# Row-tiled fill in batches 1 and 2, and moved block borders in the fill of batches 3 to 7

## The chip, the cores and the metric

The kernel runs on one core of a Trainium2 chip. The metric is device time in microseconds (us), as the median of several executions. Single slow executions (over 1.5% above the fastest of their kernel) are left out of the ratios.

## The reference

Attention with a decay of forgetting, for 8 batches of 8 heads, 576 positions and head dimension 64, feeds a two-layer network with an exact GELU.

```python
scores = matmul(q, k.T) / 8 + cum[:, None] - cum[None, :]   # cum = cumsum(log f), causal
x = softmax(scores) @ v                                     # (8, 8, 576, 64)
x = x.transpose(0, 2, 1, 3).reshape(4608, 512)
h = x @ w_in                                                # 512 -> 2048
out = gelu(h) @ w_out                                       # 2048 -> 512
```

## The kernel before

The program interleaves two things on TensorE. While the attention of batch b waits for exp on ScalarE, TensorE computes the second GEMM of batch b-1. That work is called the **fill**. A unit of fill, a step, is one contraction tile of 128 rows, taken either as one full-height matmul ("n") or as two row tiles of 64 rows ("r") that write two different banks of PSUM (the memory that TensorE writes its results to) and run side by side. The scores have 64 rows too (head dimension 64), so "r" steps stand beside scores without a change of TensorE's tiling mode. AV (the product with V), the transposes of x and the first GEMM use 128 rows.

Heads go in pairs, four pairs to a batch. A pair has four score tiles, t = 0 to 3. After each tile some fill steps are taken, and AV of the pair before comes between the tiles. There are three PSUM pools of two buffers each: "s" for scores, "o" for AV, "m" for the rest.

```python
    def scores(b, i, t):
        on_pe = b == 0 or (b == 1 and i == 0)   # causal mask as matmuls; else on GpSimd
        ...
        nc.scalar.activation(et[:, :, z:c], st[:, :, z:c], Act.Exp, scale=scale)
        for c0 in [] if on_pe else SDIAG[t]:
            nc.gpsimd.affine_select(...)

    def to_xT(b, i, copy, pool=m_psum, tag="m", ps=None):
        ...                                     # a bank ps, from the pool named
        for m in range(NBLK):
            nc.tensor.transpose(ps[:, m * P : (m + 1) * P], x_of[b, i][:, m, :, :], ident_bf)
        copy(xT(b)[:, i, :], ps)
```

The fill of batches 3 to 7 follows PLAN, token block by token block. Each block holds two banks, and ends with a copy of one and an add of the other on VectorE. FILL says how many steps follow each score tile.

```python
    PLAN = [
        (0, "o", 16 * "r"),
        (1, "m", 6 * "r" + "n" + 9 * "r"),
        (2, "m", "n" + 9 * "r" + "n" + 5 * "r"),
        (3, "s", 7 * "r" + 9 * "n"),
    ]
    FILL = [[7, 6, 3, 3], [1, 3, 3, 3], [1, 3, 3, 3], [1, 3, 3, 3], [7]]
    FILL_1 = [[0, 0, 0, 0], [0, 0, 0, 0], [2, 2, 2, 2], [2, 2, 2, 2]]   # batch 1
```

In batch 1 the fill is the first half of the contraction of two token blocks of batch 0, in full-height matmuls. The second half of that contraction comes at the start of batch 2.

```python
    def gemm2_half(c, half):
        pss = [m_psum.tile([P, d_model], FP32, tag="m", name="ps2") for _ in range(2)]
        k0, k1 = half * n_ff // 2, (half + 1) * n_ff // 2
        if half:
            order = [(ts, kt) for ts in range(2) for kt in range(k0, k1)]
        else:       # contraction tiles 0-3 of both blocks, then 4-7 of both
            order = [(ts, kq + kt) for kq in (0, 4) for ts in range(2) for kt in range(4)]
        ...         # one full-height matmul per step; evictions by VectorE and ScalarE

    def second_attention():
        ...
        for i in range(HP):
            for t in range(4):
                scores(b, i, t)
                ...
                take(fill, FILL_1[i][t])
                if i and t in (1, 2):
                    av(i - 1, t - 1)                    # one head after tile 1, one after 2
                if i > 1 and t == 0:
                    to_xT(b, i - 2, nc.vector.tensor_copy, o_psum, "o")
                ...
        to_xT(b, HP - 2, nc.vector.tensor_copy, o_psum, "o")
        av(HP - 1, 0)
        av(HP - 1, 1)
        both = s_psum.tile([P, 2, 1024], BF16, tag="s", name="ps_x2")
        gemm1_begin(1, both)                            # first GEMM starts after the last AV
        x_tail(1); load_w_out(2); load_w_out(3); load_v(2)
```

The softmax here doesn't subtract the row's maximum and nothing guards it: scores larger than these inputs give would overflow.

Of the kernel before, what the change touches and what calls it, by code (L numbers as in the profile page):

```python
# [8 lines left out]
FP32 = mybir.dt.float32  # L9
BF16 = mybir.dt.bfloat16  # L10
Act = mybir.ActivationFunctionType
Alu = mybir.AluOpType
PSUM = bass.MemoryType.PSUM

P = 128
# [37 lines left out]
def kernel(  # L53
# [214 lines left out]
    e_of = {}  # L268

    def scores(b, i, t):  # L270
        on_pe = b == 0 or (b == 1 and i == 0)
        st = s_psum.tile([P, 2, 512], FP32, tag="s", name=f"s{t}")
        c = 0
        for n, q0, w in STILES[t]:
            z = D if n == NBLK - 1 else 0
            masked = on_pe and c in SDIAG[t]
            for half in range(-1, 2 if masked else 0):
                if half == 0 and z:
                    continue
                for h in range(2):  # L280
                    d = slice(h * D, (h + 1) * D)
                    if half < 0:
                        to = st[:, h, c + z : c + w]
                        ab = kT[i][d, K0[n] : K0[n] + P], qT[i][d, q0 + z : q0 + w]
                    else:
                        last = (half + 1) * D
                        to = st[:, h, c + z : c + last]
                        ab = key_of[d, half, :], after[d, half, z:last]
                    nc.tensor.matmul(  # L289
                        to, *ab, start=half < 0, stop=half == 1 or not masked  # L290
                    )
            c += w
        z = D if t == 1 else 0
        if z:
            et = e4[(b * HP + i) % len(e4)]
        else:
            et = e_pool.tile([P, 2, 512], BF16, tag=f"e{t}", name=f"e{t}")
        e_of[b, i, t] = et
        nc.scalar.activation(et[:, :, z:c], st[:, :, z:c], Act.Exp, scale=scale)  # L299
        for c0 in [] if on_pe else SDIAG[t]:  # L300
            nc.gpsimd.affine_select(  # L301
                out=et[:, :, c0 + z : c0 + P],
                in_=et[:, :, c0 + z : c0 + P],
                compare_op=Alu.is_ge,
                fill=0.0,
                base=z,
                pattern=[[0, 2], [1, P - z]],
                channel_multiplier=-1,
            )
# [84 lines left out]
    def gemm2(c):  # L394
# [35 lines left out]

    PLAN = [
        (0, "o", 16 * "r"),
        (1, "m", 6 * "r" + "n" + 9 * "r"),
        (2, "m", "n" + 9 * "r" + "n" + 5 * "r"),
        (3, "s", 7 * "r" + 9 * "n"),
    ]

# [42 lines left out]
    def store(c, ts, ot):  # L480
        nc.sync.dma_start(out[c * S + ts * P : c * S + (ts + 1) * P, :], ot)
# [2 lines left out]

    def gemm2_half(c, half):

        pss = [
            m_psum.tile([P, d_model], FP32, tag="m", name="ps2") for _ in range(2)
        ]
        k0, k1 = half * n_ff // 2, (half + 1) * n_ff // 2  # L490
        if half:
            order = [(ts, kt) for ts in range(2) for kt in range(k0, k1)]
        else:
            order = [
                (ts, kq + kt)
                for kq in (0, 4)
                for ts in range(2)
                for kt in range(4)
            ]
        for ts, kt in order:  # L500
            nc.tensor.matmul(  # L501
                pss[ts],
                g_of[c][kt][:, ts * P : (ts + 1) * P],
                w_out_sb[:, kt, :],
                start=(kt == k0),
                stop=(kt == k1 - 1),
            )
            if kt == k1 - 1 and not half:
                ot_of.append(o_pool.tile([P, d_model], FP32, tag="ot", name="ot"))
                (nc.scalar.copy if ts else nc.vector.tensor_copy)(ot_of[ts], pss[ts])  # L510
            elif kt == k1 - 1:
                nc.vector.tensor_tensor(ot_of[ts], ot_of[ts], pss[ts], Alu.add)
                store(c, ts, ot_of[ts])
            yield

    def gemm2_third():
        yield from gemm2_half(0, 1)
        yield from gemm2_rows(0, PLAN_0)
        yield from gemm2_rows(1, PLAN_1)

    def take(gen, n):
# [92 lines left out]



    FILL = [[7, 6, 3, 3], [1, 3, 3, 3], [1, 3, 3, 3], [1, 3, 3, 3], [7]]
    FILL_2 = [[8, 8, 8, 8], [8, 8, 4, 4], [4, 4, 4, 4], [4, 4, 4, 4], [8]]
    FILL_1 = [[0, 0, 0, 0], [0, 0, 0, 0], [2, 2, 2, 2], [2, 2, 2, 2]]

    def attention(b):

# [33 lines left out]
    def second_attention():  # L656
# [16 lines left out]
        for i in range(HP):  # L673
            for t in range(4):
# [1 line left out]
                if i == 0 and t < 3:  # L676
                    transposes(t + 1, *((m_psum, "m") if t == 1 else (o_psum, "o")))
                take(fill, FILL_1[i][t])
                if i and t in (1, 2):
                    av(i - 1, t - 1)  # L680
                if i > 1 and t == 0:
                    to_xT(b, i - 2, nc.vector.tensor_copy, o_psum, "o")
                if (i, t) == (1, 3):
                    load_qk_tokens(2, which="k")
                if (i, t) == (3, 0):
                    transpose_dma(2, 0, 4)
                    transpose_dma(2, 4, 8)
        to_xT(b, HP - 2, nc.vector.tensor_copy, o_psum, "o")
        av(HP - 1, 0)
        av(HP - 1, 1)  # L690
        both = s_psum.tile([P, 2, 1024], BF16, tag="s", name="ps_x2")
        gemm1_begin(1, both)
        x_tail(1)
        load_w_out(2)
        load_w_out(3)
# [66 lines left out]
```

## Time and profile before

The median is 348.33 us (347.60 to 348.62, four executions); the profiled span is 345.7 us. The table gives the lengths of the batches in the trace, from the first score matmul of one to that of the next.

| stretch | before, us |
|---|---|
| batch 1 | 32.60 |
| batch 2 | 46.91 |
| each of batches 3 to 7, mean | 36.15 |

The end of batch 1's attention shows where its waits are. This is the timeline of TensorE: start, length, line, tiles, count, and in brackets idle time with its releaser. In all views PE is TensorE, PEld its weight loads, DVE VectorE, ACT ScalarE, POOL GpSimd and SP SyncE.

```profile
47.07 0.37 PE L289 MATMUL s<-qT,kT 64*128 64x256 bf16 x4 [0.28 <-ACT e L299]
...
55.26 0.31 PE L289 MATMUL s<-qT,kT 64*128 64x320 bf16 x2
...
56.91 0.97 PE L320 MATMUL o<-vw,e 128*128 128x65 bf16 x25 [0.15 <-POOL e L301]
...
72.27 0.37 PE L289 MATMUL s<-qT,kT 64*128 64x256 bf16 x4
```

The first line is the start of pair 2, the second the last score tile of pair 3, the third the last AV waiting for the mask on GpSimd, and the fourth the start of batch 2.

### The profile page before, as it was taken

Reading aid. Unit: us, or ns where it says so; the run is one execution under the profiler, and the core shown is the slowest. Engines: PE = TensorE matmul, PEld = TensorE weight load, DVE = VectorE, ACT = ScalarE, POOL = GpSimd, SP = SyncE. Lnnn points to the kernel's source line nnn. Section 1 sums busy time; section 2 is a strip of 40 time slices with the busy share of each in tenths; the row PEclk is TensorE's granted clock in tenths of the full one; section 3 lists DMA queues with packets and bytes.
Section 4 is the critical chain, followed back from the end, with each engine's and each line's share of the span. In section 5 each row is a group of like instructions: output and inputs, shape, how many; then the busy total and the mean of one; then the engine's idle time right before and its main releaser. Section 6 shows DMA issues by size and latency. Waiting matters only on the chain.

```text
span 345.7 us, 7895 instructions
## 1 busy us (share of the span) xinstructions
PE 328.3 (95%) x3187; PEld 173.7 (50%) x3227; DVE 188.1 (54%) x424; ACT 212.1 (61%) x296; POOL 125.1 (36%) x256
## 2 busy tenths in 40 slices
PE   7899999999999999999899989998999899999995
PEld 3674555445554455545554555445544554444443
DVE  5670456934367935795479647974597542020011
ACT  5976786773634787368746874687468765503600
POOL 8390673128418044533345333624261430000000
PEclk9999999999999999999999999999999999999999
DMA  8999999979992999488935995498900230011013
GB/s 116 176 171 194 202 178 147 170 149 161 222 183 100 138 202 176 81 119 167 219 89 81 134 211 137 74 161 190 170 30 2 69 83 30 2 61 61 0 35 89
DMA packets 99924, 43.03 MB, mean 124 GB/s; under 512 B 78704, under 2 KB 95344, under 8 KB 99888
## 3 DMA queue, kind: packets, MB, share of 16 engines
q1 hardware_dynamic: 82592, 28.37, 42.4%
q0 software_dynamic: 16896, 13.63, 26.9%
q8 instruction: 25, 0.41, 0.5%
q10 hardware_dynamic: 400, 0.52, 0.4%
q14 instruction: 11, 0.09, 0.1%
HBM read 36.85 MB, written 9.44 MB: 134 GB/s over the span
## 4 chain that ended last, share of the span: by engine, by line
PE 89%; DVE 4%; ACT 3%; issue 2%; POOL 2%; POOLq 0%; ACTq 0%; DVEq 0%
PE ps L375 35%; PE ps L466 25%; PE o L320 9%; PE ps L408 8%; PE s L289 8%; ACT e L299 2%; PE ps L501 2%; PE ps_x L353 1%; DVE ot L474 1%; PE ps_f L206 1%; DVE x L334 1%; POOL q L107 1%; POOL k L107 1%; DVE qT L213 0%; DVE kT L213 0%
## 5 line engine op out<-in xcount | busy, mean ns | idle before, releaser
L392 ACT ACTIVATE g<-ps 128x512 bf16<-128x512 f32 x144 | 85.3, 597 | 80.2 <-PE ps L375 80.2
L299 ACT ACTIVATE e<-s 128x896 bf16<-128x896 f32 (+2 forms) x128 | 101.0, 836 | 32.1 <-PE s L289 28.2
L375 PE MATMUL ps<-xT,w_in_sb 128*128 128x512 bf16 x497 | 111.4, 379 | 0.8
L466 PE MATMUL ps<-w_out_sb,g 64*128 64x512 bf16 (+1 forms) x736 | 104.0, 376 | 4.7 <-DVE ot L474 3.9
L375 PEld LDWEIGHTS <-w_in_sb 128*128 128x128 bf16 x576 | 56.0, 98 | 67.5 <-issue 1.8
L301 POOL TENSOR_SCALAR_AFFINE_SELECT e<-e 128x256 bf16<-128x256 bf16 (+1 forms) x135 | 49.5, 385 | 100.1 <-ACT e L299 99.9
L466 PEld LDWEIGHTS <-g 64*128 64x128 bf16 (+1 forms) x756 | 39.8, 94 | 40.4 <-issue 10.6
L244 DVE COPY qT<-tq 64x288 bf16<-64x288 bf16 x96 | 49.3, 514 | 1.4
L260 POOL TENSOR_TENSOR vw<-v_sb,wT 128x640 bf16<-128x640 f32 x31 | 39.6, 1279 | 24.7 <-DMA v_sb<-in_v_dram 24.5
L289 PE MATMUL s<-qT,kT 64*128 64x320 bf16 (+4 forms) x384 | 43.9, 277 | 3.3 <-ACT e L299 2.6
L320 PE MATMUL o<-vw,e 128*128 128x65 bf16 x960 | 36.8, 194 | 2.7 <-issue 2.4
L320 PEld LDWEIGHTS <-e 128*128 128x128 bf16 x960 | 34.8, 98 | 9.2 <-POOL e L301 4.1
L474 DVE COPY ot<-ps 128x512 f32<-128x512 f32 x26 | 17.9, 690 | 35.5 <-PE ps L466 35.5
L244 DVE COPY kT<-tk 64x288 bf16<-64x288 bf16 x96 | 33.0, 344 | 1.6
L334 DVE TENSOR_TENSOR x<-o,r 128x320 bf16<-128x320 f32 x64 | 31.5, 492 | 2.2
L417 DVE COPY ot<-ps 128x512 f32<-128x512 f32 (+2 forms) x9 | 5.7, 632 | 48.8 <-PE ps L408 31.9
L289 PEld LDWEIGHTS <-kT 64*128 64x128 bf16 x384 | 18.7, 94 | 22.6 <-issue 7.3
L333 DVE RECIPROCAL r<-o 128x5 f32<-128x5 f32 x64 | 12.2, 190 | 30.8 <-PE o L320 30.7
L408 PE MATMUL ps<-w_out_sb,g 128*128 128x512 bf16 (+2 forms) x142 | 27.9, 355 | 0.1
L408 PEld LDWEIGHTS <-g 128*128 128x128 bf16 x144 | 13.5, 98 | 14.5
L476 DVE TENSOR_TENSOR ot<-ot,ps 128x512 f32<-128x512 f32 x26 | 17.9, 687 | 1.2
L375 PE MATMUL ps<-tails,w_in_sb 128*128 128x512 bf16 x63 | 14.3, 377 | 0.1
(64 smaller groups left out, 148.2 us busy)
## 6 DMA issues: line engine op xcount, KB each, us to landing
out_dram<-ot SPq DMA_DIRECT2D x32, 256.0 KB, 2.3
v_sb<-in_v_dram SPq DMA_DIRECT2D x24, 256.0 KB, 5.7
q<-in_q_dram POOLq DMA_DIRECT2D x6, 576.0 KB, 6.2
k<-in_k_dram POOLq DMA_DIRECT2D x6, 576.0 KB, 8.2
v_sb<-in_v_dram SPq DMA_DIRECT2D x22, 128.0 KB, 5.3
w_in_sb<-in_moe_w_in_dram POOLq DMA_DIRECT2D x4, 512.0 KB, 7.0
w_out_sb<-in_moe_w_out_dram POOLq DMA_DIRECT2D x4, 512.0 KB, 8.4
q<-in_q_dram POOLq DMA_DIRECT2D x4, 144.0 KB, 4.5
```

Source lines behind the costliest of these rows:

```text
L244: nc.vector.tensor_copy(rows[:, odd], src[odd * D : (odd + 1) * D, 2 * i + h].rearrange("d j p -> d p j"),)
L260: eng.tensor_tensor(vw_of[b][:, hs, :, 0:D], v_sb[:, hs, :, :], w.unsqueeze(3).to_broadcast([P, 2, NBLK, D]), Alu.mult,)
L289: nc.tensor.matmul(to, *ab, start=half < 0, stop=half == 1 or not masked)
L299: nc.scalar.activation(et[:, :, z:c], st[:, :, z:c], Act.Exp, scale=scale)
L301: nc.gpsimd.affine_select(out=et[:, :, c0 + z : c0 + P], in_=et[:, :, c0 + z : c0 + P], compare_op=Alu.is_ge, fill=0.0, base=z, pattern=[[ ...
L320: nc.tensor.matmul(o[:, m, :], e_of[b, i, t][:, h, c : c + P], vw_of[b][:, 2 * i + h, n, :], start=(n == 0), stop=(n == m),)
L334: nc.vector.tensor_tensor(x_of[b, i][:, :, h, :], o[:, :, 0:D], r.unsqueeze(2).to_broadcast([P, NBLK, D]), Alu.mult,)
L375: nc.tensor.matmul(ps, w_in_sb[:, kt, ffb * P : (ffb + 1) * P], src[:, kt, 0:TC], start=(kt == 0), stop=(kt == n_dm - 1),)
L392: nc.scalar.activation(g_of[c][ffb], ps, Act.Gelu)
L408: nc.tensor.matmul(pss[ts][:, c0:c1], g_of[c][kt][:, ts * P : (ts + 1) * P], w_out_sb[:, kt, c0:c1], start=(kt == 0), stop=(kt == n_ff - 1),)
L466: nc.tensor.matmul(banks[r], g_of[c][kt][rows, ts * P : (ts + 1) * P], w_out_sb[rows, kt, :], start=kt == (steps.index("r") if r else 0), ...
L474: nc.vector.tensor_copy(ot, banks[1])
```

## The change

It has three parts. (a) In the steady fill (batches 3 to 7) the borders of the token blocks move to the AV runs, so that the eviction of a finished block lies under AV. (b) In batch 2 the second half of the split contraction becomes row tiles, and the order of its blocks changes. (c) In batch 1 the fill becomes row tiles too. So that AV and the transposes stand together in 128-row mode, both heads' AV and the x transpose move to tile 2; the last mask goes from GpSimd to TensorE; and four matmuls of the first GEMM are begun ahead of the last AV.

```diff
--- before.py
+++ after.py
@@ -268,7 +268,7 @@
     e_of = {}
 
     def scores(b, i, t):
-        on_pe = b == 0 or (b == 1 and i == 0)
+        on_pe = b == 0 or (b == 1 and (i == 0 or (i, t) == (HP - 1, 3)))
         st = s_psum.tile([P, 2, 512], FP32, tag="s", name=f"s{t}")
         c = 0
         for n, q0, w in STILES[t]:
@@ -430,8 +430,8 @@
 
     PLAN = [
         (0, "o", 16 * "r"),
-        (1, "m", 6 * "r" + "n" + 9 * "r"),
-        (2, "m", "n" + 9 * "r" + "n" + 5 * "r"),
+        (1, "m", 6 * "r" + "n" + 8 * "r" + "n"),
+        (2, "m", 9 * "r" + "n" + 6 * "r"),
         (3, "s", 7 * "r" + 9 * "n"),
     ]
 
@@ -484,38 +484,42 @@
 
     def gemm2_half(c, half):
 
-        pss = [
-            m_psum.tile([P, d_model], FP32, tag="m", name="ps2") for _ in range(2)
-        ]
+
         k0, k1 = half * n_ff // 2, (half + 1) * n_ff // 2
-        if half:
-            order = [(ts, kt) for ts in range(2) for kt in range(k0, k1)]
-        else:
-            order = [
-                (ts, kq + kt)
-                for kq in (0, 4)
-                for ts in range(2)
-                for kt in range(4)
+        for ts in range(2):
+            pool, held = (o_psum, "o") if half and ts else (m_psum, "m")
+            banks = [
+                pool.tile([P, d_model], FP32, tag=held, name="ps2") for _ in range(2)
             ]
-        for ts, kt in order:
-            nc.tensor.matmul(
-                pss[ts],
-                g_of[c][kt][:, ts * P : (ts + 1) * P],
-                w_out_sb[:, kt, :],
-                start=(kt == k0),
-                stop=(kt == k1 - 1),
-            )
-            if kt == k1 - 1 and not half:
-                ot_of.append(o_pool.tile([P, d_model], FP32, tag="ot", name="ot"))
-                (nc.scalar.copy if ts else nc.vector.tensor_copy)(ot_of[ts], pss[ts])
-            elif kt == k1 - 1:
-                nc.vector.tensor_tensor(ot_of[ts], ot_of[ts], pss[ts], Alu.add)
-                store(c, ts, ot_of[ts])
-            yield
+            for kt in range(k0, k1):
+                for r in range(2):
+                    rows = slice(r * D, (r + 1) * D)
+                    nc.tensor.matmul(
+                        banks[r],
+                        g_of[c][kt][rows, ts * P : (ts + 1) * P],
+                        w_out_sb[rows, kt, :],
+                        start=(kt == k0),
+                        stop=(kt == k1 - 1),
+                    )
+                if kt == k1 - 1:
+                    if not half:
+                        ot_of.append(
+                            o_pool.tile([P, d_model], FP32, tag="ot", name="ot")
+                        )
+                        nc.vector.tensor_copy(ot_of[ts], banks[0])
+                    else:
+                        nc.vector.tensor_tensor(
+                            ot_of[ts], ot_of[ts], banks[0], Alu.add
+                        )
+                    nc.vector.tensor_tensor(ot_of[ts], ot_of[ts], banks[1], Alu.add)
+                    if half:
+                        store(c, ts, ot_of[ts])
+                yield
 
     def gemm2_third():
+        yield from gemm2_rows(0, PLAN_0[:1])
         yield from gemm2_half(0, 1)
-        yield from gemm2_rows(0, PLAN_0)
+        yield from gemm2_rows(0, PLAN_0[1:])
         yield from gemm2_rows(1, PLAN_1)
 
     def take(gen, n):
@@ -614,9 +618,9 @@
 
 
 
-    FILL = [[7, 6, 3, 3], [1, 3, 3, 3], [1, 3, 3, 3], [1, 3, 3, 3], [7]]
+    FILL = [[7, 6, 3, 3], [1, 3, 3, 2], [1, 3, 3, 3], [1, 3, 3, 3], [8]]
     FILL_2 = [[8, 8, 8, 8], [8, 8, 4, 4], [4, 4, 4, 4], [4, 4, 4, 4], [8]]
-    FILL_1 = [[0, 0, 0, 0], [0, 0, 0, 0], [2, 2, 2, 2], [2, 2, 2, 2]]
+    FILL_1 = [[0, 0, 0, 0], [0, 0, 0, 2], [2, 2, 2, 2], [2, 2, 2, 0]]
 
     def attention(b):
 
@@ -676,20 +680,36 @@
                 if i == 0 and t < 3:
                     transposes(t + 1, *((m_psum, "m") if t == 1 else (o_psum, "o")))
                 take(fill, FILL_1[i][t])
-                if i and t in (1, 2):
-                    av(i - 1, t - 1)
-                if i > 1 and t == 0:
+                if i == 1 and t in (1, 2):
+                    av(0, t - 1)
+                if i > 1 and t == 2:
                     to_xT(b, i - 2, nc.vector.tensor_copy, o_psum, "o")
+                    av(i - 1, 0)
+                    av(i - 1, 1)
                 if (i, t) == (1, 3):
                     load_qk_tokens(2, which="k")
                 if (i, t) == (3, 0):
                     transpose_dma(2, 0, 4)
                     transpose_dma(2, 4, 8)
-        to_xT(b, HP - 2, nc.vector.tensor_copy, o_psum, "o")
+        pss = [gemm1(1, ffb, (0, 1)) for ffb in range(2)]
         av(HP - 1, 0)
         av(HP - 1, 1)
         both = s_psum.tile([P, 2, 1024], BF16, tag="s", name="ps_x2")
-        gemm1_begin(1, both)
+        to_xT(1, HP - 2, nc.vector.tensor_copy, ps=both[:, 0, 0:XC])
+        more = s_psum.tile([P, 2, 512], FP32, tag="s", name="ps1")
+        pss += [more[:, 0, :], more[:, 1, :]]
+        gemm1(1, 2, (0, 1), pss[2])
+        for ffb in range(2):
+            gemm1(1, ffb, (2,), pss[ffb])
+        gemm1(1, 2, (2,), pss[2])
+        to_xT(1, HP - 1, nc.vector.tensor_copy, ps=both[:, 1, 0:XC])
+        gemm1(1, 3, (0, 1, 2), pss[3])
+        for ffb in range(2):
+            gemm1(1, ffb, (3,), pss[ffb])
+        for ffb in (2, 3):
+            gemm1(1, ffb, (3,), pss[ffb], False)
+        gelu(1, 2, pss[2])
+        gelu(1, 3, pss[3])
         x_tail(1)
         load_w_out(2)
         load_w_out(3)
```

## The prediction

> **What bounds the kernel now.** I read the page first (busy shares, chain, groups), then the waits, then the chain in order of time, then the timeline of the stretches that the diff touches.
>
> ```profile
> PE 328.3 (95%) x3187; PEld 173.7 (50%) x3227; DVE 188.1 (54%) x424; ACT 212.1 (61%) x296; POOL 125.1 (36%) x256
> ...
> PE 89%; DVE 4%; ACT 3%; issue 2%; POOL 2%; POOLq 0%; ACTq 0%; DVEq 0%
> ...
> L466 PE MATMUL ps<-w_out_sb,g 64*128 64x512 bf16 (+1 forms) x736 | 104.0, 376 | 4.7 <-DVE ot L474 3.9
> ```
>
> TensorE is the bound; the clock row is 9 throughout. The change deletes no arithmetic: it can win only idle time and mode switches of TensorE. The fill row names one idle time that repeats: 3.9 us behind the eviction of L474, five times in the waits. One of the five, in batch 3 (timeline, TensorE and then VectorE):
>
> ```profile
> 128.39 0.33 PE L289 MATMUL s<-qT,kT 64*128 64x64 bf16 x4
> 128.55 0.60 PE L466 MATMUL ps<-w_out_sb,g 64*128 64x512 bf16 x4
> 129.93 0.38 PE L466 MATMUL ps<-w_out_sb,g 128*128 128x512 bf16 x1 [0.79 <-DVE ot L474]
> 130.15 1.11 PE L320 MATMUL o<-vw,e 128*128 128x65 bf16 x30
> 131.19 0.36 PE L289 MATMUL s<-qT,kT 64*128 64x448 bf16 x2
> ...
> 129.19 0.69 DVE L474 COPY ot<-ps 128x512 f32<-128x512 f32 x1 [1.86 <-PE ps L466]
> 129.91 0.69 DVE L476 TENSOR_TENSOR ot<-ot,ps 128x512 f32<-128x512 f32 x1
> ```
>
> The last row-tile pair of a token block ends, the next block's first matmul wants the same bank, and the bank is free only after the copy ends at 129.88. Batch 1 looks different: it switches between 64-row and 128-row work all the time.
>
> ```profile
> 49.47 0.36 PE L289 MATMUL s<-qT,kT 64*128 64x448 bf16 x2
> 49.76 0.60 PE L501 MATMUL ps<-w_out_sb,g 128*128 128x512 bf16 x2
> 50.21 0.63 PE L320 MATMUL o<-vw,e 128*128 128x65 bf16 x15
> 50.77 0.31 PE L289 MATMUL s<-qT,kT 64*128 64x320 bf16 x2
> 51.01 0.60 PE L501 MATMUL ps<-w_out_sb,g 128*128 128x512 bf16 x2
> ```
>
> The 448-column scores hold TensorE 0.19 us when 64-row fill follows (126.35 to 126.55 in batch 3), here 0.29: a switch costs 0.10. A row-tile pair and one full-height matmul cost the same 0.216.
>
> **What the Trainium skill says.** "TensorEngine Tiling", Key Properties: changing the tiling mode drains TensorE; the trace agrees, 0.10 us each. Same page, Gotcha 1: different row tiles write different PSUM banks. So each row-tiled block has two banks and two evictions; the trace agrees (0.69 + 0.69 us). "TensorE: Matmul & The Clock Gate", Part 1, engine queue depths: VectorE is a strict FIFO. The rows above are in program order; I lean on this. "Perfetto Trace Analysis", Optimization Strategy: a gap that repeats can mean that there isn't enough PSUM for the next tile. That is this wait.
>
> **The change part by part.**
>
> (a) Steady fill, batches 3 to 7. Block 1 now ends with its full-height matmul just ahead of AV (the attention-times-V run), so its eviction lies under AV. Old cost: pairs end at 128.55 + 4 x 0.108 = 128.98, the matmul could start after a switch at 129.09 and starts at 129.93: 0.84. Two smaller waits appear. (1) Fill in pair 1, tile 3 falls from 3 steps to 2, so the next two score tiles come 0.216 earlier. The second needs the bank of an exp that ends at 128.32: it can start at 128.37, against 128.17 for TensorE: 0.20. (2) Block 2 starts after AV and one score tile. From the end of the last pair, x = 128.96: copy at x + 0.21, add at x + 0.93 to x + 1.62, bank free x + 1.67; TensorE is there at x + 0.32 (switch, matmul) + 0.95 (AV) + 0.10 + 0.19 = x + 1.56: 0.1. Net 0.84 - 0.30 = 0.54 a batch, times 5 = **-2.7 us**. (The step moved to the end, 8 for 7, is work and cancels.)
>
> (b) Batch 2's second half of the token blocks of batch 0 turns to row tiles. Before, 8 full-height matmuls stood after each of two score tiles, four switches (74.30 to 74.40 and so on); now none until AV: 4 x 0.105 = **-0.4 us**. The new order, one block in the o banks first, puts off the need for the last quarters of w_out by 1.9 us.
>
> (c) Batch 1. Won: eight switches per pair become two (in, out), twice 6 x 0.105 = 1.3 us. The wait for the last exp and mask (55.93 to 56.9, about 0.7 with the piece inside AV) is hidden by 4 matmuls of the first GEMM; the mask's 0.41 us on GpSimd becomes under 0.1 us on TensorE.
> Lost: I laid the new order on these durations from 46.62, where the orders part.
> - The second quarter of w_out lands at 39.48 + 8.9 = 48.4 (longest of the two transfers, below). The old order took contraction tiles 0 to 3 of both blocks first and needed tile 4 at 53; the new one needs it at 47.85. Wait **0.55**.
>
> ```profile
> L173 POOL DMA_DIRECT2D w_out_sb<-in_moe_w_out_dram x2: 755/786/818, 38.7 to 39.5; - x2
> ...
> DMA to landing us min/median/max: 6.7/7.8/8.9
> ```
>
> - In pairs 2 and 3 the x transpose now stands directly ahead of both AV runs, and all three use the pool of two o banks. The instruction order of the changed kernel shows the second head's first AV matmul waiting for VectorE, and by the count it is the copy out of the transpose's bank. VectorE does that third: copy and add of the fill block just ended, then the xT copy. From the fill's end y: y + 0.21 + 0.72 + 0.61 + 0.49 = y + 2.03, plus 0.05. TensorE: switch 0.10, transposes 0.28, first head 0.47: y + 0.86. Wait **1.2**, twice = **2.4**.
> - After AV, the third GEMM step needs the xT copy of pair 2, which queues behind the normalisation of both heads of pair 3 (end of AV + 0.2 + 0.21 + 0.49 + 0.49): wait about **0.7**. Small ones (xT of pair 3, first gelus) 0.25.
> Laid out whole, 52 matmuls of the first GEMM remain at 62.5; they end at 62.5 + 52 x 0.216 + 0.15 = 73.9. Before, GEMM ended at 72.25. So batch 1 is **+1.6 us** (+0.5 to +2.3).
>
> Sum: 348.35 - 2.7 - 0.4 + 1.6 = **346.8**.
>
> **The rivals.** (R1) The o-bank wait in batch 1 isn't there or is short, and batch 1 wins about 1 us: 344.3. For it: the author meant it so, and every switch removed is real. Against: the wait in the instruction order, and VectorE's FIFO. (R2) The early part is bound by transfers: the DMA engines are at 9 tenths from 62 to 73 us, v of batch 2 lands at 68.6 + 6.6 = 75.2, GpSimd then needs 7 us of weighing before its masks, and in the kernel before the last mask comes just in time for AV at 84.2. Then any gain before 84 us is lost there: R1 would give 345.3. With batch 1 later, as I expect, this doesn't bind; the last quarters of w_out start later (about 62.9 against 60.25) and are needed at 76 to 77: enough. (R3) ScalarE becomes the bound of the steady attention: 3.26 us of exp in 4.0 us of a pair leaves 0.74, so only the 0.2 at one tile, counted above. If neither small wait showed, (a) would be -4.2 and the time 345.3.
>
> **Range and chances.** My two large terms have opposite signs, each sure to about 1 us; the mean is 346.8, the range 345.0 to 348.4. Faster by 2% means under 341.4: 7 us, more than all idle that the change can reach (0.84 x 5 + 0.4 + about 2.5 in batch 1 = 7.1), so 0.02. Slower by 2% is 355.3: 0.01. Within 2%: 0.97.
>
> **What would show it.** (a) The waits of fill matmuls on L474 fall from 3.9 us to about 0.5, about 0.1 behind the add of L476, and 0.2 per batch of scores behind exp; a steady batch, 36.2 us before (193.55 - 157.39), takes 35.6. (b) Batch 2 from its first score to its first AV is 0.4 shorter. (c) In batch 1, AV waits about 1.2 us behind DVE xT twice, the fill waits for w_out near 48 us, and batch 2's first scores start at 73.9, not 72.27. If AV shows no such wait, my reading of the banks is wrong, and R1 holds; if batch 2's AV waits on masks, R2.

## More of the kernel before

The windows view of the kernel before, for batches 1, 2 and 3. The columns are the window and its length, then busy time (and instructions) of TensorE, its weight loads, VectorE, ScalarE and GpSimd, then the granted clock, the share of the DMA engines (over 1 where transfers overlap) and GB/s.

```profile
39.67:72.27 32.60, 30.94 (x354) 17.22 (x359) 22.66 (x59) 24.77 (x36) 13.98 (x27) 1.00 1.14 178
72.27:119.18 46.91, 45.99 (x429) 22.95 (x436) 27.17 (x59) 25.41 (x34) 22.15 (x41) 1.00 0.88 159
119.18:155.34 36.16, 34.79 (x349) 18.56 (x353) 24.83 (x55) 24.64 (x34) 15.20 (x31) 1.00 0.82 138
```

Window length less TensorE's busy time is what a reordering can still win: 1.7 us in batch 1, 1.4 us in a steady batch, plus what mode switches cost inside "busy".

## The result

Both kernels give correct results. The ratio is the mean time of one kernel's fast runs over that of the other's in the same rounds, so it is not quite the ratio of the medians.

| | before | after |
|---|---|---|
| median, us (range; executions) | 348.33 (347.60 to 348.62; 4) | 347.81 (347.61 to 348.59; 4) |
| ratio (95% interval) | | 0.9992 (0.9971 to 1.0014) |
| profiled span, us | 345.7 | 345.5 |
| batch 1, us | 32.60 | 35.43 |
| batch 2, us | 46.91 | 46.49 |
| each of batches 3 to 7, mean, us | 36.15 | 35.65 |

The time is the same: the interval holds 1. But the trace isn't the same. Batch 1 takes 2.83 us more, batch 2 takes 0.42 us less, and five steady batches take 0.50 us less each. The sum is 2.83 - 0.42 - 5 x 0.50 = -0.09 us: the last part starts at 299.83 us instead of 299.92.

From the page of the kernel after: the busy shares, the chain that ended last, and the group of fill matmuls (busy time, mean ns, idle time ahead of them).

```profile
PE 327.5 (95%) x3219; PEld 175.2 (51%) x3263; DVE 192.4 (56%) x429; ACT 211.4 (61%) x295; POOL 124.3 (36%) x255
...
PE 80%; DMA 9%; POOL 4%; issue 3%; DVE 2%; SPq 1%; ACT 1%; POOLq 0%; DVEq 0%
...
L466 PE MATMUL ps<-w_out_sb,g 64*128 64x512 bf16 (+1 forms) x731 | 103.0, 376 | 0.8 <-issue 0.8
```

The idle time ahead of the fill, 4.7 us before, is 0.8 us, and the eviction of L474 is no longer its cause. (The 0.8 us is most likely missing records: in e15's trace of the same kernel, with 756 records of this group instead of 731, it is 0.0.) In the chain a DMA has appeared with 9%; where it comes from is shown below. The windows view after, for the same three batches:

```profile
39.67:75.10 35.43, 30.39 (x375) 17.67 (x379) 25.08 (x61) 23.88 (x35) 15.10 (x30) 1.00 1.11 172
75.10:121.59 46.49, 45.58 (x445) 23.19 (x452) 30.24 (x65) 25.40 (x34) 20.77 (x40) 1.00 0.85 155
121.59:157.26 35.67, 34.92 (x349) 18.74 (x355) 23.94 (x54) 24.68 (x34) 15.15 (x31) 1.00 0.73 139
```

In batch 1 TensorE is idle for 5.0 us instead of 1.7 (a few missing matmul records count as idle in both). The timeline of TensorE after, at the same marks and at the waits between them:

```profile
47.07 0.37 PE L289 MATMUL s<-qT,kT 64*128 64x256 bf16 x4
...
47.69 0.34 PE L289 MATMUL s<-qT,kT 64*128 64x64 bf16 x4
48.95 0.61 PE L497 MATMUL ps<-w_out_sb,g 64*128 64x512 bf16 x4 [0.91 <-DMA w_out_sb<-in_moe_w_out_dram]
...
50.40 0.64 PE L320 MATMUL o<-vw,e 128*128 128x65 bf16 x15
52.13 0.63 PE L320 MATMUL o<-vw,e 128*128 128x65 bf16 x15 [1.09 <-DVE xT L356]
...
57.45 0.64 PE L320 MATMUL o<-vw,e 128*128 128x65 bf16 x15 [1.10 <-DVE xT L356]
58.02 0.31 PE L289 MATMUL s<-qT,kT 64*128 64x320 bf16 x2
...
59.22 1.11 PE L320 MATMUL o<-vw,e 128*128 128x65 bf16 x30
60.17 0.44 PE L353 MATMUL ps_x<-ident_bf,x 128*128 128x128 bf16 x5
...
61.69 0.81 PE L375 MATMUL ps<-xT,w_in_sb 128*128 128x512 bf16 x3 [0.65 <-DVE xT L356]
...
75.10 0.36 PE L289 MATMUL s<-qT,kT 64*128 64x256 bf16 x4
```

A transfer holds the fill, then the second head's AV waits for the xT copy in pair 2 and again in pair 3, and the first GEMM waits for the next xT copy. The brackets count only the time in which no matmul was in flight. The delay of the work is measured from start to start: the second head starts 1.73 us after the first. Without a wait 15 such matmuls take 0.48 us (the 30 of the last AV run take 0.95 us, from 59.22 to the transposes at 60.17), so the delay is 1.25 us. VectorE in the same stretch shows why:

```profile
50.19 0.69 DVE L509 COPY ot<-ps 128x512 f32<-128x512 f32 x1 [2.88 <-PE ps L497]
50.99 0.69 DVE L514 TENSOR_TENSOR ot<-ot,ps 128x512 f32<-128x512 f32 x1
51.59 0.48 DVE L356 COPY xT<-ps_x 128x640 bf16<-128x640 bf16 x1
```

The transposes hold one of the two "o" banks and the first head the other. The second head needs the transposes' bank. The copy that frees it (L356) stands in VectorE's queue behind the two evictions of the fill block, and ends at 52.07; AV starts at 52.13.

The chain that ended last (start, length, what) shows what the transfer of w_out hung on:

```profile
24.09 13.28 DMA v_sb<-in_v_dram
...
37.54 1.27 POOL vw L260
...
39.72 9.18 DMA w_out_sb<-in_moe_w_out_dram
```

GpSimd issues the loads of w_out behind the weighing of V, and that waits until V of batch 1 has landed. So the second quarter was issued at 39.72 us and landed at 48.9. Over all 17 traces it was issued between 38.5 and 40.8 us and landed 8.7 to 9.5 us later, between 47.3 and 50.0 us. This path is part of the 9% of DMA in the chain.

**Where batch 1's 2.83 us come from.** From pair 2's first scores (47.07 in both kernels) to pair 3's last ones the kernel before takes 8.19 us and the kernel after 10.95 us, with 14 fill steps in each: 2.76 us more. By starts, the w_out wait is 1.10 (fill 1.26 us after its scores, where 0.16 is usual), the two AV waits are 2 x 1.25 = 2.50, and one score tile starts 0.64 us after the fill ahead of it instead of 0.43, while ScalarE runs its exps without a gap: 0.21. That makes 3.81. So the rest of the stretch won 3.81 - 2.76 = 1.05 us: this is what the removed mode switches brought. By the order of the work they are ten: in pair 2 two are left of eight, in pair 3 three of seven, since the tail behind pair 3 uses 128 rows in both kernels. Ten switches at 0.105 us are 1.05 us. From there to batch 2 it is 17.01 us before and 17.08 after, although two fill steps (0.43 us) have left that stretch. The wait for the xT copy (0.81 us by starts) and small ones took what the earlier mask and the begun GEMM gave.

### The profile page after: what moved, and what is told of

Same layout as the page of the kernel before. It is cut to its first block, busy times and chain, and to the rows that moved or that the text cites. A ratio compares the mean times of both kernels' runs of the same rounds, so it can differ in the third digit from the quotient of the medians.

```text
span 345.5 us, 7975 instructions
## 1 busy us (share of the span) xinstructions
PE 327.5 (95%) x3219; PEld 175.2 (51%) x3263; DVE 192.4 (56%) x429; ACT 211.4 (61%) x295; POOL 124.3 (36%) x255
## 4 chain that ended last, share of the span: by engine, by line
PE 80%; DMA 9%; POOL 4%; issue 3%; DVE 2%; SPq 1%; ACT 1%; POOLq 0%; DVEq 0%
PE ps L375 31%; PE ps L466 25%; PE ps L408 8%; PE o L320 8%; PE s L289 6%; DMA v_sb<-in_v_dram 6%; DMA w_out_sb<-in_moe_w_out_dram 3%; PE ps L497 2%; POOL vw L260 1%; SPq L119 1%; ACT g L392 1%; PE ps_x L353 1%; POOL q L107 1%; DVE x L334 1%; POOL k L107 1%
## 5 line engine op out<-in xcount | busy, mean ns | idle before, releaser
L301 POOL TENSOR_SCALAR_AFFINE_SELECT e<-e 128x256 bf16<-128x256 bf16 (+1 forms) x134 | 48.8, 383 | 102.5 <-ACT e L299 102.2
L466 PEld LDWEIGHTS <-g 64*128 64x128 bf16 (+1 forms) x756 | 41.4, 94 | 40.2 <-issue 11.9
L244 DVE COPY qT<-tq 64x288 bf16<-64x288 bf16 x96 | 48.9, 509 | 1.4
L289 PE MATMUL s<-qT,kT 64*128 64x320 bf16 (+4 forms) x384 | 45.7, 276 | 3.4 <-ACT e L299 2.4
L474 DVE COPY ot<-ps 128x512 f32<-128x512 f32 x26 | 17.9, 689 | 36.6 <-PE ps L466 36.6
L244 DVE COPY kT<-tk 64x288 bf16<-64x288 bf16 x96 | 35.0, 364 | 1.6
L289 PEld LDWEIGHTS <-kT 64*128 64x128 bf16 x384 | 20.1, 94 | 23.0 <-issue 8.0
L365 POOL COPY tails<-xT 128x256 bf16<-128x256 bf16 x8 | 3.2, 402 | 33.7 <-DVE xT L356 33.7
```

The lines of the kernel that those rows point to most:

```text
L244: nc.vector.tensor_copy(rows[:, odd], src[odd * D : (odd + 1) * D, 2 * i + h].rearrange("d j p -> d p j"),)
L289: nc.tensor.matmul(to, *ab, start=half < 0, stop=half == 1 or not masked)
L301: nc.gpsimd.affine_select(out=et[:, :, c0 + z : c0 + P], in_=et[:, :, c0 + z : c0 + P], compare_op=Alu.is_ge, fill=0.0, base=z, pattern=[[ ...
L466: nc.tensor.matmul(banks[r], g_of[c][kt][rows, ts * P : (ts + 1) * P], w_out_sb[rows, kt, :], start=kt == (steps.index("r") if r else 0), ...
L474: nc.vector.tensor_copy(ot, banks[1])
```

## The experiments

All were timed in five rounds beside the kernel before (medians of it 348.3, 348.22, 348.07 and 347.97 us in the four groups of runs). Changes in us are against the kernel before, worked out as (ratio - 1) x that median. On this scale the kernel after is at -0.3 us in its own rounds and at +0.2 us in those of e15; many expectations count from it instead. The ratios leave slow executions out, but the medians of e2, e4 and e11 still hold one each. e13 to e15 ran on another chip than e1 to e12.

### Each part alone

**e1: the steady fill alone.** The kernel before, with the new PLAN and FILL only.

```diff
-        (1, "m", 6 * "r" + "n" + 9 * "r"),
-        (2, "m", "n" + 9 * "r" + "n" + 5 * "r"),
+        (1, "m", 6 * "r" + "n" + 8 * "r" + "n"),
+        (2, "m", 9 * "r" + "n" + 6 * "r"),
-    FILL = [[7, 6, 3, 3], [1, 3, 3, 3], ..., [7]]
+    FILL = [[7, 6, 3, 3], [1, 3, 3, 2], ..., [8]]
```

> The kernel before with the changed plan and fill counts of the steady batches 3 to 7 alone. My theory (the parts add up; this one is worth what the traces show per batch, 36.17 to 35.67 us, five times): 2.5 us faster than before, 345.8 us, ratio 0.993. Rival (the steady part is worth little, and what looks like a gain is only the start of the batch moved): within 0.5 us of before.

Measured: 346.33 us, ratio 0.9944 (0.9921 to 0.9967), so -1.95 us. In its trace a steady batch is 35.65 us long in the mean, 0.50 us less. Part (a) is worth what its mechanism says; its expected 2.5 us lies inside the interval (1.1 to 2.8).

**e2: batch 2 alone.** The kernel before, with the row-tiled second half and the new order of blocks.

```diff
+        yield from gemm2_rows(0, PLAN_0[:1])
         yield from gemm2_half(0, 1)            # as row tiles
-        yield from gemm2_rows(0, PLAN_0)
+        yield from gemm2_rows(0, PLAN_0[1:])
```

> The kernel before with the row-tiled second half of batch 0's token blocks and its new order in batch 2 alone. Theory that four mode switches are all that counts: 0.4 us faster. Rival R2 of the prediction (batch 2's first AV waits for GpSimd, which waits for the transfer of v): the gain ends at the first AV, whose masks come at the same time as before (84.2 us); then 0 to 0.15 us faster and a wait of about 0.3 us of AV behind the masks in the trace.

Measured: 347.68 us (347.52 without the slow execution), ratio 0.9976 (0.9959 to 0.9993), -0.84 us; the 0.4 us expected lies inside the interval. Its profiled execution was a slow one and is not used for the sum. In that execution V of batch 2 landed late (GpSimd could start on it at 78.76 us, 75.40 in the kernel before), and AV then waited for the masks on GpSimd.

**e3: batch 1 alone.** The kernel before, with part (c): the row-tiled first half, FILL_1, the new second_attention and the mask of the last tile.

```diff
-    FILL_1 = [[0, 0, 0, 0], [0, 0, 0, 0], [2, 2, 2, 2], [2, 2, 2, 2]]
+    FILL_1 = [[0, 0, 0, 0], [0, 0, 0, 2], [2, 2, 2, 2], [2, 2, 2, 0]]
-                if i and t in (1, 2):
-                    av(i - 1, t - 1)
+                if i > 1 and t == 2:
+                    to_xT(b, i - 2, nc.vector.tensor_copy, o_psum, "o")
+                    av(i - 1, 0)
+                    av(i - 1, 1)
   ... (and the other lines of this part)
```

> The kernel before with the batch 1 part alone (row tiles from the second pair on, the x transposes ahead of both AV runs, first GEMM ahead of the last AV, last mask on the tensor engine). My theory: this part costs what the trace of the changed kernel shows, batch 2's first scores at 75.1 instead of 72.3 us, so 2.8 us slower, 351.1 us; AV waits 1.1 us twice behind the xT copy, the fill about 0.9 us for w_out. Rival: the batch 1 part wins about 1 us by itself (fewer mode switches) and loses only together with the others: 347.3 us.

Measured: 350.34 us, ratio 1.0058 (1.0042 to 1.0074), +2.0 us. The interval excludes zero: part (c) costs time. In its trace batch 1 is 34.98 us long (+2.4), with the same two AV waits and a w_out wait of 0.45 us.

**e4: everything but batch 1.** The kernel after, with the old batch 1.

```diff
-        b, fill = 1, gemm2_half(0, 0)
+        b, fill = 1, gemm2_half_old(0, 0)   # full-height, as before
   ... (old FILL_1, old order in second_attention, old mask)
```

> The changed kernel with the batch 1 part undone. If the parts add up: 2.8 us faster than the changed kernel, 2.9 us faster than before, 345.4 us. If R2 holds (batch 2's first AV bound by the masks when batch 1 ends early): 0.3 us less gain, 345.7 us. If batch 1's part is not the loss: about 347.8 us, as the changed kernel.

Measured: 345.10 us (344.90 without the one slow execution), ratio 0.9912 (0.9890 to 0.9935), -3.1 us. The kernel after shows -0.3 us in its own rounds. So parts (a) and (b) together are worth about 3 us, and part (c) gives nearly all of it back.

### What batch 1 waits for

**e5: the transposes away from AV.** The kernel after, with the x transpose of pairs 2 and 3 back at tile 0.

```diff
+                if i > 1 and t == 0:
+                    to_xT(b, i - 2, nc.vector.tensor_copy, o_psum, "o")
                 if i > 1 and t == 2:
-                    to_xT(b, i - 2, nc.vector.tensor_copy, o_psum, "o")
                     av(i - 1, 0)
```

> The changed kernel with the two x transposes of batch 1 moved back to the first score tile of each pair, so that the copy out of their o bank is long done when the second head's AV wants it. Theory (AV waits for a bank whose copy queues behind the two evictions): both waits of 1.1 us go, two more mode switches per pair (0.2 us) come: 1.8 us faster than the changed kernel, 346.0 us. Rival (AV would wait for something else at the same place, exp or masks): less than 0.5 us faster.

Measured: 346.53 us, ratio 0.9945 (0.9908 to 0.9982), -1.9 us, which is 1.6 us better than the kernel after where 1.8 was expected, with a wide scatter (344.88 to 349.32). Both AV waits are gone from the trace, and batch 1 takes 32.70 us. This shows the cause of the two waits: the place of the transposes in the queue for the "o" banks. But batch 2 now takes 48.21 us instead of 46.49. Its timelines of TensorE and then GpSimd:

```profile
84.89 0.24 PE L320 MATMUL o<-vw,e 128*128 128x65 bf16 x2 [0.40 <-POOL e L301]
85.86 1.33 PE L320 MATMUL o<-vw,e 128*128 128x65 bf16 x28 [0.73 <-POOL e L301]
...
77.33 1.28 POOL L260 TENSOR_TENSOR vw<-v_sb,wT 128x640 bf16<-128x640 f32 x1 [14.31 <-DMA v_sb<-in_v_dram]
```

GpSimd waits for V until 77.33, then weighs V, issues two loads, and only then makes the masks that AV needs. This is rival R2 of the prediction: when TensorE reaches batch 2 earlier, it can meet this bound. In the kernel after, TensorE came too late to meet it.

**e6: the first GELUs later.** The kernel after, with the GELUs of two tiles issued after the tiles 5 and 7 of the first GEMM, instead of four in a burst.

```diff
-        gelu(1, 2, pss[2])
-        gelu(1, 3, pss[3])
+        late_gelus.extend(((2, pss[2]), (3, pss[3])))
         ...
             gemm1(b, ffb)
+            if b == 1 and ffb in (5, 7):
+                gelu(1, *late_gelus.pop(0))
```

> The changed kernel with the gelus of tiles 2 and 3 of batch 1's first GEMM issued behind those of tiles 5 and 7. Theory (tiles 0 to 3 end within 0.9 us, their four gelus queue on ScalarE, and tile 6 waits for a bank behind them): the tensor engine's 0.4 us of waits right after 63.4 us go, 0.4 us faster than the changed kernel. Rival (that lost time is the tensor engine's own, records apart): no change.

Measured: 348.31 us, ratio 1.0001 (0.9978 to 1.0024): no gain, against the kernel after either. From the last transposes to batch 2 the trace goes from 12.76 to 12.64 us only. The burst is real and costs little; the expected 0.4 us was wrong.

**e7: no wait for w_out.** A wrong result (relative error 0.175): the first half reads the first quarter of w_out twice, so that it never needs the second quarter.

```diff
-                        w_out_sb[rows, kt, :],
+                        w_out_sb[rows, kt if half else kt % 4, :],
```

> The changed kernel, giving a wrong result on purpose: the first half of batch 0's second-GEMM fill in batch 1 reads the first quarter of w_out in place of the second, so it need not wait for the second quarter to land. Theory (the fill waits for that transfer from 47.85 to about 48.9 us): the wait goes, about 0.2 us of it comes back as scores waiting for exp; 0.9 us faster than the changed kernel, 346.9 us. Rival (the pairs of batch 1 are paced by exp anyway): under 0.3 us.

Measured: 347.58 us, ratio 0.9975 (0.9957 to 0.9992), -0.9 us. That is 0.6 us better than the kernel after, not the 0.9 expected, and the two intervals overlap, so the times do not decide. Nor does the trace: batch 1 takes 34.57 us, 0.86 less than in the first trace of the kernel after, but here w_out landed at 47.9 us, ahead of the need at 48.26, and the unedited kernel takes the same 34.57 in e15 below. That the wait is real rests on the first trace of the kernel after and on e3. By starts it is 1.10 us there, and its absence is worth less, 0.86, because another score tile then waits 0.2 us for exp, which e15 shows.

**e13: none of the three.** Wrong in the same way: e5, e6 and e7 together.

> The changed kernel with all three suspected waits of batch 1 taken away at once: x transposes early (e5), gelus late (e6), first quarter of w_out read twice (e7, so a wrong result on purpose). If these waits are the whole loss, batch 1 from its first scores to batch 2's takes about 32.2 us (35.4 less 2 x 0.9, 0.9 and 0.4; before: 32.6), and the time is 345.1 us where the transfer of v comes in time. If something else in the new batch 1 costs as well (row tiles themselves, the second bank's eviction), batch 1 stays 0.5 us or more above the 32.6 us of before.

Measured: 346.17 us, ratio 0.9951 (0.9934 to 0.9968), -1.7 us. Batch 1 takes 32.68 us, against 32.60 us in the kernel before. So without these waits the new order is level with the old one, not better. The run does not separate the three: w_out landed at 48.3 us, ahead of its need at 48.70, and e5 alone already had 32.70 us, also without a w_out wait. The wait for the xT copy ahead of the first GEMM is still there (0.57 us in brackets), and no run removed it. The timeline says where the rest of the gain went. With the transposes at tile 0, each pair has two switches more (the fill ahead of the transposes takes 0.53 us instead of 0.43, the scores behind them start after 0.39 instead of 0.29): 0.4 us in two pairs. And the first fill steps after AV take 0.66 us instead of 0.43, because the add that frees their bank ends at 51.44. That wait lay hidden under the AV wait in the kernel after.

**e14: another grouping of the fill.** e5, with the fill steps of pair 2 moved towards tile 2, so that the second quarter of w_out is needed later.

```diff
-    FILL_1 = [..., [2, 2, 2, 2], [2, 2, 2, 0]]
+    FILL_1 = [..., [1, 1, 4, 2], [2, 2, 2, 0]]
```

> e5 with batch 1's fill regrouped (1, 1, 4, 2 steps in pair 2 in place of 2, 2, 2, 2), so that the second quarter of w_out is needed about 0.6 us later, with a right result. Theory: no wait for that transfer in any run, and the scores of pair 2 come earlier: batch 1 takes 33.0 us or less, 346 us or a little under; e5's profile had 32.7. Rival: ScalarE paces pair 2, and the lost fill shows as scores waiting for exp: 0.3 us slower than e5.

Measured: 347.04 us, ratio 0.9965 (0.9945 to 0.9986), -1.2 us; batch 1 is 32.83 us with no w_out wait. But w_out landed at 48.2 us here, and by e5's order (8.7 us after the start of batch 1, at 40.47) it would have been needed at 49.2 only, so this trace does not test the regrouping. The interval overlaps that of e5, so nothing is decided; there is no sign of a gain.

**e15: the changed kernel again.** No edit, in the same rounds as e13 and e14.

> The changed kernel itself once more, in the same rounds as e13 and e14. If my account holds (steady -2.5, batch 2 -0.4, batch 1 +2.0 without the wait for w_out and up to +2.8 with it): 347.4 to 348.2 us, 0 to 0.9 us under before. In its profile the fill's wait for w_out may be there or not (0.9 us in the first profile, 0.45 in e3, none in e6 and e8, whose batch 1 began 0.1 to 0.7 us later).

Measured: 348.18 us, ratio 1.0007 (0.9988 to 1.0025). The result of the first rounds holds. Its trace has the two AV waits (1.10 and 1.10 in brackets) and the xT wait (0.65), and no w_out wait: the second quarter landed at 47.8 us instead of 48.9, and batch 1 began at 40.59 instead of 39.67, so that TensorE took it up at 48.78. Either alone would have removed nearly all of the wait, as the need was at 47.85 in the first trace. Batch 1 takes 34.57 us here, +1.97. In e6, too, batch 1 began late (40.36) and the quarter landed early (48.2). The w_out wait is a race between GpSimd's issue with its transfer and TensorE, and an execution that is late at batch 1's start does not lose that time a second time.

### The steady fill, and a better kernel

**e8: the remaining small waits of part (a).** The kernel after, with the full-height step of block 1 placed one earlier and the short tile moved from tile 3 to tile 1 of pair 1.

```diff
-        (1, "m", 6 * "r" + "n" + 8 * "r" + "n"),
+        (1, "m", 5 * "r" + "n" + 9 * "r" + "n"),
-    FILL = [[7, 6, 3, 3], [1, 3, 3, 2], ...]
+    FILL = [[7, 6, 3, 3], [1, 2, 3, 3], ...]
```

> The changed kernel with the step of fill that pair 1 gave up in its last tile taken from its second tile instead (before the first AV), the full-height step moved along. Theory (in the steady batches the scores of pair 2 wait 0.2 us for the exp of pair 1 because the tensor engine comes one step early): that wait goes in five batches, 1.0 us faster than the changed kernel, 346.8 us; the AV run of pair 0 still finds its masks done. Rival (the wait moves to the first AV, behind the mask of pair 0's last tile): no change.

Measured: 346.78 us, ratio 0.9964 (0.9941 to 0.9987), -1.25 us, 1.0 us better than the kernel after in its own rounds (-0.28). In the trace four of the five steady batches take 35.4 to 35.5 us instead of 35.67; 5 x 0.22 = 1.1 us. One took 36.2 in this execution. The small waits that it removes are seen in the steady timeline of the kernel after (batch 3, TensorE):

```profile
130.19 0.37 PE L289 MATMUL s<-qT,kT 64*128 64x256 bf16 x4
130.38 0.40 PE L466 MATMUL ps<-w_out_sb,g 64*128 64x512 bf16 x2
130.79 0.34 PE L289 MATMUL s<-qT,kT 64*128 64x64 bf16 x4
...
131.72 1.11 PE L320 MATMUL o<-vw,e 128*128 128x65 bf16 x30 [0.16 <-issue]
132.76 0.36 PE L289 MATMUL s<-qT,kT 64*128 64x448 bf16 x2
132.96 0.97 PE L466 MATMUL ps<-w_out_sb,g 64*128 64x512 bf16 x6
```

The 64-column scores start at 130.79, 0.41 us after the fill pair ahead of them, where the pair takes 0.21: 0.20 us behind exp, with no bracket, since the pair's records overlap the wait. The six matmuls at 132.96 take 0.97 us where e9 below takes 0.81 at the same place: they wait for the bank of the block's add.

**e9: the old batch 1 with a tuned steady fill.** e4, with two full-height steps at the end of block 1, so that the copy can start earlier.

```diff
+        (1, "m", 5 * "r" + "n" + 8 * "r" + 2 * "n"),
+    FILL = [[7, 6, 3, 3], [1, 2, 3, 3], ..., [8]]
```

> The kernel e4 (changed kernel, batch 1 undone) with the fill step moved as in e8 and the block that ends at the second AV closing with two full-height matmuls, so that its last row-tile pair, and with it the eviction, comes 0.22 us earlier. Theory: 345.1 us less 1.0 (e8) less 0.14 us in five batches, 0.7 (the bank of the block's add no longer holds up the next block) = 343.4 us; a steady batch takes 35.3 us. Rival: the early eviction changes nothing and 0.2 us of scores waiting for exp returns: 344.3 us.

Measured: **343.77 us** (342.83 to 346.98), ratio 0.9866 (0.9812 to 0.9920), -4.7 us. It beats both kernels, with correct results. A steady batch takes 35.3 us. Its page has no idle time ahead of the fill at all:

```profile
L466 PE MATMUL ps<-w_out_sb,g 64*128 64x512 bf16 (+1 forms) x751 | 109.2, 377 | 0.0
```

**e10: a tail of batch 1 with the good parts of (c).** e9, with the last mask on TensorE and two matmuls of the first GEMM ahead of the last transposes.

```diff
+        ps0 = gemm1(1, 0, (0, 1))
         to_xT(b, HP - 2, nc.vector.tensor_copy, o_psum, "o")
         av(HP - 1, 0)
         av(HP - 1, 1)
   ... (then the rest of gemm1_begin, reordered)
```

> e9 with only the end of batch 1 changed: last mask on the tensor engine, two matmuls of the first GEMM ahead of the last x transpose and AV. Theory of the tensor engine as the bound: 0.6 us less than e9, 342.8 us, batch 2's first scores 0.6 us earlier. Rival R2 (batch 2's first AV waits for its masks, these for the transfer of v): the 0.6 us are lost again at that AV: as e9, with AV waiting on GpSimd in the trace.

Measured: 343.61 us, ratio 0.9865 (0.9812 to 0.9917): the same as e9. Batch 1 is 32.36 us instead of 32.60, 0.24 of the 0.6 us expected, which is too little for these rounds to tell.

**e11: q and k of batch 3 loaded later.** e10, with that issue behind the first masks of batch 2, so that GpSimd makes its masks earlier.

```diff
-                if ffb == (9 if b == 1 else 14):
+                if b > 1 and ffb == 14:
                     load_qk_tokens(b + 2)
+                if b == 2 and (i, t) == (0, 3):
+                    load_qk_tokens(3)
```

> e10 with GpSimd's two issues of batch 3's q and k loads (1.6 us of its time) moved from before the masks of batch 2's first pair to behind them. R2: the masks come 1.6 us earlier, AV no longer waits, 342.8 us and less spread between runs than e10. Rival (R2 plays no part): the same as e10; if the loads are then too late for batch 3's transposes, slower.

Measured: 345.39 us (345.07 without the one slow execution), ratio 0.9906 (0.9847 to 0.9964). By the medians of the fast executions it is 1.5 us slower than e10; the intervals overlap. It does not help.

**e12: the same edit on e5.**

> e5 with the same move of the q and k loads. e5's runs fell into two groups, 344.9 to 345.9 and 347.2 to 349.3 us, and its profile, of the second group, had batch 2's first AV waiting 1.1 us for masks. If R2 makes the groups: all runs at 345 to 346 us, mean 1 us under e5's. If the groups come from elsewhere (transfers of the first 40 us): two groups again.

Measured: 348.00 us, ratio 0.9986 (0.9937 to 1.0034). A miss. AV no longer waits for the masks, but the fill waits elsewhere (timelines of TensorE and then VectorE):

```profile
99.02 0.37 PE L466 MATMUL ps<-w_out_sb,g 64*128 64x512 bf16 x1 [2.45 <-DVE ot L474]
...
98.27 0.69 DVE L474 COPY ot<-ps 128x512 f32<-128x512 f32 x1 [6.00 <-DMA out_dram<-ot]
```

An eviction waits 6 us for an earlier block's store to land and free its target. The stores are issued by SyncEngine, which at that time issues the transposes of batch 3's q (from 93.86 for 5.10 us), late because q was loaded late. That the store stood behind them is the likely reading; it was not tested. Batch 2 takes 51.56 us. The old place of these loads was better.

## Why the prediction was right or wrong

The prediction named a net gain of 1.5 us. None was measured beyond the noise. 347.81 us lies in the range, but the forecast of a gain was wrong. **The step that failed is the size of (c)**, "So batch 1 is +1.6 us": it measured +2.83 us with the w_out wait and +1.97 without it. Its mechanisms were right but for one uncounted wait; the terms that were mis-sized are the transfer of w_out (0.55 forecast, 1.10 measured) and the switches won (1.3 forecast, 1.05 measured). As (c) stood against -3.1 us of the other two parts, the miss of 1.23 us is most of the 1.5 us that were forecast; (a) makes up 0.2 more.

- **(a) was right.** Forecast 0.54 us a batch and 2.7 in sum, measured 0.50 and 2.5. The wait on L474 is gone. Both smaller waits are there: 0.20 us of scores behind exp as forecast, and 0.16 us (0.97 against 0.81) behind the add, forecast 0.1. e8 and e9 remove them and win what they are worth. (The x = 128.96 of its working should be 128.98, as it says further up; the offsets are right.)
- **(b) was right in mechanism and size.** 0.4 forecast, 0.42 in the trace; e2's -0.84 agrees within its interval. The Trainium skill, "TensorEngine Tiling (Array Packing)", Key Properties, says that a change of the tiling mode drains TensorE; the trace agrees here (four switches fewer, 0.42 us).
- **(c), the wait for the "o" bank: right.** "Wait 1.2, twice" measured 1.25 and 1.25 us by starts. e5 removed it by moving the transposes alone, so the cause is shown. That VectorE is a strict FIFO (the Trainium skill, "TensorE: Matmul & The Clock Gate", Part 1, engine queue depths) is what puts L356 behind L509 and L514. The trace agrees: the three run in the order of the program.
- **(c), the transfer of w_out: mechanism right, size uncertain.** The need at 47.85 was right. The transfer allowed the fill at 48.95, not at 48.4, so 1.10 us by starts instead of 0.55. But it was no fixed cost: e3 had 0.45 in brackets, e6 and e15 had none. One landing time of the kernel before (48.4), carried to another execution, could not give this term to better than 1 us: over the traces the quarter landed between 47.3 and 50.0 us, since GpSimd's issue waits for V.
- **(c), the switches won: too large.** "Twice 6 x 0.105 = 1.3" measured 1.05. The price was right, also behind AV: 30 AV matmuls take 1.04 us to the next scores (131.72 to 132.76 above) and 0.95 to the transposes. The count was wrong: only pair 2 loses six switches. Pair 3 goes from seven to three, because the first GEMM behind it needs 128 rows in both kernels, so ten go and not twelve.
- **(c), left out.** One score tile waits 0.21 us for exp in the row-tiled part; with the w_out wait absent there are two. The prediction had counted this kind of wait in (a) and not looked for it in (c).
- **(c), the tail.** xT was forecast at 0.7 and took 0.65 in brackets, 0.81 by starts. The "small ones 0.25" were about 0.5 (17.08 us, less 15.8 for the matmuls at their own spacing and 0.81 for xT), and e6 shows that the burst of GELUs is only about 0.1 of it.

These add up. Of the 1.23 us by which batch 1 was missed, w_out is 0.55, the switches 0.25, the exp wait 0.21, the two AV waits 0.1, and about 0.1 is left for the tail. (The terms listed in the prediction add up to +1.9, not +1.6; the two fill steps, 0.43 us, that in the timeline after fit ahead of 47.07, where the kernel before waits for exp, are not among them.)

**The rivals.** R1 (no bank wait, so batch 1 wins about 1 us) is refuted by e3 and by the waits themselves; e13 shows more: even without the waits that it removed, batch 1 wins nothing. R2 (V, GpSimd and the masks bound the start of batch 2) did not bind in the changed kernel, since batch 1 ended late, as forecast; e5 shows that it is real. R3 (ScalarE) binds only at single tiles.

**What stays open.** Why the start of batch 1 (39.7 to 42.6 us over all traces) and the landing of single transfers differ by up to a few microseconds between executions was not tested; for w_out the chain leads back to the landing of V of batch 1, and no further run looked there. An earlier issue of w_out, ahead of that weighing, was not tried. Nor is it known how often the w_out wait occurs in executions that were not profiled. In e5, why V landed as late as 77.33 is not settled. And no version was found in which the row-tiled batch 1 beats the old one.

## What to carry to other kernels

A block border of accumulated work is free where the next work uses other banks, so put it just ahead of such a run and keep an eviction's worth of time on either side. When work is moved to spare mode switches, follow each bank that it takes to the instruction that frees it, and count what stands ahead of that instruction on its engine: here 1.4 us of evictions ahead of one copy, in two pairs, cost 2.5 us, more than the 1.05 us that all the switches saved. A net forecast from two opposite terms is only as good as the worse of them, so count the switches on both orders of work, and follow a transfer back to what its issue waits for, before adding them up.

## What the Trainium skill lacked or had wrong

- "TensorEngine Tiling (Array Packing)", Key Properties, says that a change of the mode drains TensorE, without a cost. The runs show 0.10 us where 128-row fill follows scores (0.29 us instead of 0.19), and about as much where scores follow a run of AV (1.04 us instead of 0.95).
- "TensorE: Matmul & The Clock Gate", Back-to-back issue gap, gives a sustained rate of about 131 ns for a matmul of 512 columns. In the kernel before, the last 60 such matmuls of batch 1's first GEMM (one record is missing) took 13.14 us, a switch at the end included, and 8 of the fill took 1.83 us to the next scores: 0.217 and 0.216 us each. The 216 ns that the page gives for the isolated gap is what the streams here showed.
- "Perfetto Trace Analysis" does not say that a trace can lack records of matmuls: the fill group has 731 to 756 records of the same instruction count in different traces. Counts and idle times of small groups are to be read with that in mind.
- "DMA: Bandwidth & Descriptors" gives no spread of a transfer's time between executions of one kernel: the second quarter of w_out landed 8.7 to 9.5 us after its issue in 17 traces.
